# A long convolution and a gated feed-forward on one core: the second transform stage as sixteen array tiles, with a stored instruction order

## The chip, the cores and the metric

The kernel runs on one core of one Trainium2 chip. The time is the device time of one execution, in microseconds (us). Before the change it was 329.91 us, the median of three runs (324.05 to 332.69).

The core has five engines with a queue each, run in order: TensorE (PE in the profile; PEld are its weight loads), VectorE (DVE), ScalarE (ACT), GpSimd (POOL) and SyncE (SP). PE writes to PSUM, eight banks of 512 float32 per partition; the kernel uses them as four tiles of two banks. DMAs are issued from the queues of SP, ACT and POOL.

## What is computed

2048 positions, 640 channels, F = 1728. Inputs and output are bfloat16. `B_x` is not used.

```python
x = A_q
k_shift[s] = sum over t of k[s - t] * shift_k[:, t]        # 4 taps per channel
kv = k_shift * v
y  = irfft(rfft(pad(kv)) * rfft(pad(ssm_k)))[:2048]        # causal long convolution, per channel
y  = y + kv * ssm_D
h  = x + layernorm(x) * y
g, u = silu(layernorm(h) @ w_gate), layernorm(h) @ w_up
out = h + (g * u) @ w_down
```

## The kernel before

**Blocks.** The sequence is cut into four blocks of 512 positions (`j` = 0 to 3). Position 4p + b of a block lies in partition p, column group b, so a block is four row groups (`b`) of 128 partitions. The channels are cut into two halves (`c`) of 320 columns (`CW`). The convolution is done block against block by a transform of 1024 points, so that output block j is the sum over i of the spectrum of x-block i times the spectrum of filter block j - i. The feed-forward part of block j needs the whole convolution of block j.

**Block 0** (`dense_c`): both transforms are dense. `dense_h` multiplies by 128x128 matrices from a table of 2 MB (`den`), eight matmuls of 320 columns for each of four frequency groups `h`; `products` and `combine` make the complex product on DVE, and eight more matmuls per `h` transform back.

**Blocks 1 to 3** (`conv_c`): `kv_block` makes the taps and the product with v on DVE, eight instructions of 1280 columns per half. `fwd` is the first transform stage (two 128x128 matmuls per `b`), whose result goes through four SBUF-to-SBUF DMAs that regroup the partitions. `spec` (with `stage2`) is the second stage: per `h` and operand four matmuls of 128 rows by 64 columns. `shift_add` (two DVE instructions of 640) adds the spectrum of the filter block before. `products` multiplies the complex spectra, with pairs of 1280-column instructions for each term and adds between the terms; `combine` and, in block 3, two further adds finish real and imaginary parts. `inv2` is the inverse second stage (64 rows by 128 columns), followed by an evacuation, a regrouping DMA (`rs`) and the inverse first stage in `conv_bp`, which also multiplies with the normalised x, adds x and takes the statistics of the second layernorm. Each `evac` of 640 columns from PSUM may run on ACT or DVE.

**Feed-forward.** `ffn_pair` multiplies by `WG` and `WU` (540 matmuls of 512 columns over the four blocks), takes silu on ACT and the product on DVE straight from PSUM. `ffn_b` multiplies by `WD` (448 matmuls of 320 columns); for blocks 0 and 1 x is added on PE by 16 identity matmuls (`RESPE`) and the result evacuated, for blocks 2 and 3 DVE adds it.

**Order.** `P.op` only lists the operations with a priority and an estimated cost. `Prog.schedule` then walks a simulated clock and fixes the order on each engine, and for operations that ACT or DVE may do, the engine; `emit` writes the five queues with their semaphore waits. Loads of blocks 1 to 3 and of the weights are issued on POOL's queue (`load_kv`, `load_x`, `load_weights`); a weight piece waits until the piece two before it has landed, and the first ones until `kv_last[0, 0]`, the last tap instruction of block 0. `KIN` and `VIN` have one buffer each, so the load for a next half waits for the instructions that read the one before. The regrouping DMAs are on SP's queue. For blocks 1 to 3 the filter is turned by a DMA transpose through DRAM.

All PE operations but transposes are recorded by the helper in line 559, all DVE two-operand instructions by line 756, evacuations by 542 (with a scale: 545), DMA issues by line 550; silu is line 1103, normalisation 876 and 877, the layernorm sums on ACT 889 and 896, the power on POOL 867.

Of the kernel before, what the change touches and what calls it, by code (L numbers as in the profile page):

```python
# [40 lines left out]
class Prog:  # L41
    ENG = ("pe", "act", "dve", "pool", "sp")
    FRESH = {"pe": 0.22, "act": 0.145, "dve": 0.125, "pool": 0.15, "sp": 0.1}
    OVERLAP = {"pe": 0.0, "act": 0.105, "dve": 0.085, "pool": 0.0, "sp": 0.0}
    WIN = 3.41333

# [62 lines left out]
    def pe_end(self, t, c):  # L109

        w = self.clock
        while c > 1e-12:
            k = int((t + 1.7 + 1e-7) // self.WIN)
            while w["k"] < k:
                u = w["busy"].get(w["k"], 0.0) / self.WIN
                if w["s"] == 1.0:
                    if u < 0.55 and w["k"] > 8:
                        w["s"] = 0.5
                elif u >= 0.83:
                    w["s"] = 1.0  # L120
                w["k"] += 1
            e = (k + 1) * self.WIN - 1.7
            if e - t < 1e-9:
                e += self.WIN
            d = min(c / w["s"], e - t)
            w["busy"][k] = w["busy"].get(k, 0.0) + d
            t += d
            c -= d * w["s"]
        return t

    def schedule(self, dma_model, bias):
        self.clock = {"k": -1, "s": 1.0, "busy": {}}
        pemode = 0
        free = {e: 0.0 for e in self.ENG}
        order = {e: [] for e in self.ENG}
        ready = []
        for o in self.ops:
            o.ready = o.minready
            if o.npred == 0:
                ready.append(o)  # L140
        dmafree = [0.0]
        t = 0.0
        left = len(self.ops)
        while left:
            done_any = True
            while done_any:
                done_any = False
                for e in ("pe", "dve", "act", "sp", "pool"):
                    if free[e] > t + 1e-9:
                        continue  # L150
                    best, held = None, set()
                    for o in sorted((o for o in ready if e in o.engs and o.ready <= t + 1e-9), key=lambda o: (o.prio, o.idx)):
                        c = o.engs[e]
                        if e == "dve" and "act" in o.engs:
                            if max(t, free["act"]) + o.engs["act"] <= t + c + bias:
                                continue
                        if e == "act" and "dve" in o.engs:
                            if max(t, free["dve"]) + o.engs["dve"] + bias < t + c:
                                continue
                        ok = True  # L160
                        want = {}
                        for tl in o.tiles:
                            if tl.live:
                                continue
                            pl = self.pools[tl.pool]
                            n = want.get(tl.pool, 0)
                            if pl.inorder and (pl.at + n >= len(pl.seq) or pl.seq[pl.at + n] is not tl):
                                ok = False
                                break
                            if tl.pool in held:  # L170
                                ok = False
                                break
                            want[tl.pool] = n + 1
                        if not ok:
                            continue
                        for pn, n in want.items():
                            if sum(1 for f in self.pools[pn].free if f[0] <= t + 1e-9) < n:
                                ok = False
                                if n > 1:
                                    held.add(pn)  # L180
                        if ok:
                            best = o
                            break
                    if best is None:
                        continue
                    o = best
                    done_any = True
                    ready.remove(o)
                    left -= 1
                    for tl in o.tiles:  # L190
                        if not tl.live:
                            pl = self.pools[tl.pool]
                            pl.free.sort(key=lambda f: f[0])
                            _, tl.base, tl.prev = pl.free.pop(0)
                            tl.live = True
                            if pl.inorder:
                                pl.at += 1
                    o.eng, o.start = e, t
                    if o.dma is None:
                        c = o.engs[e] - self.OVERLAP[e]  # L200
                        if e == "pe":
                            c += 0.105 if o.mode != pemode else 0.0
                            pemode = o.mode
                        o.finish = self.pe_end(t, c) if e == "pe" else t + c
                        free[e] = o.finish
                    else:
                        free[e] = t + o.engs[e]
                        o.finish = dma_model(o, free[e], dmafree)
                    o.pos = len(order[e])
                    order[e].append(o)  # L210
                    for tl in o.tiles:
                        tl.touch.append(o)
                        tl.left -= 1
                        if tl.left == 0 and tl.pool is not None:
                            self.pools[tl.pool].free.append((max(p.finish for p in tl.touch) + 0.14, tl.base, tl.touch))
                    for s in o.succ:
                        s.npred -= 1
                        k = s.deps[o]
                        if k == 0 or (e == "pe" and "pe" in s.engs):
                            fin = o.finish  # L220
                        else:
                            fin = o.finish + max(self.FRESH[x] for x in s.engs)
                        s.ready = max(s.ready, fin)
                        if s.npred == 0:
                            ready.append(s)
            nxt = [f for f in free.values() if f > t + 1e-9] + [o.ready for o in ready if o.ready > t + 1e-9]
            for pl in self.pools.values():
                nxt += [f[0] for f in pl.free if f[0] > t + 1e-9]
            if not nxt:
                if left:  # L230
                    raise RuntimeError("stuck: " + "; ".join(
                        f"{o.name}[{','.join(x.name for x in o.tiles if not x.live)}]" for o in ready[:20]))
                break
            t = min(nxt)
        self.order = order
        self.span = max(o.finish for o in self.ops)

    def emit(self, nc, es, block, ndma_sems):
        sems = {e: es.enter_context(nc.semaphore("s_" + e)) for e in self.ENG}
        dsem = [[es.enter_context(nc.semaphore(f"s_d{i}")), 0, None, i < ndma_sems[0]] for i in range(sum(ndma_sems))]  # L240
        glob = sorted(self.ops, key=lambda o: (o.start, o.idx))
# [102 lines left out]
def _tables(R):  # L344
    N = 256 * R
    I1 = 64 // R
    q = np.arange(128)[:, None]
    s1f = np.zeros((128, 2, 128))
    for T in range(2):
        f1 = (64 * T + np.arange(64))[None, :] + 0.5  # L350
        s1f[:, T, 0:64] = np.cos(2 * np.pi * q * f1 / 256)
        s1f[:, T, 64:128] = -np.sin(2 * np.pi * q * f1 / 256)
    s1i = np.stack([s1f[:, T, :].T for T in range(2)], axis=1)
    w2 = np.zeros((2, R, 128, 2, 64))
    w2i = np.zeros((128, R, 2, 128))
    for T in range(2):
        for G in range(R):
            for i in range(I1):
                f1 = 64 * T + R * i + G + 0.5
                for m in range(R):  # L360
                    col = i * R + m
                    for b in range(R):
                        r0, r1 = i * R + b, 64 + i * R + b
                        th = 2 * np.pi * b * (f1 + 256 * m) / N
                        w2[T, G, r0, 0, col] = np.cos(th)
                        w2[T, G, r1, 0, col] = np.sin(th)
                        w2[T, G, r0, 1, col] = -np.sin(th)
                        w2[T, G, r1, 1, col] = np.cos(th)
            w2i[T * 64:(T + 1) * 64, G, 0, :] = w2[T, G, :, 0, :].T
            w2i[T * 64:(T + 1) * 64, G, 1, :] = w2[T, G, :, 1, :].T  # L370
# [33 lines left out]
def bass_sequential_preLN__ssm_conv_h3__swiglu_ffn__prompt_kernel(  # L404
# [27 lines left out]
    with ExitStack() as es:  # L432
# [98 lines left out]
        def dve4(n):  # L531
            return 0.274 + 0.00026 * n
# [706 lines left out]
```

## Time and profile before

One profiled execution had a span of 329.1 us; the median of the plain runs is 329.91 us.

| engine | busy us | share | instructions |
|---|---|---|---|
| PE | 284.9 | 87% | 1724 |
| DVE | 251.0 | 76% | 441 |
| ACT | 184.7 | 56% | 293 |
| POOL | 40.8 | 12% | 55 |

| instructions | count | mean ns |
|---|---|---|
| DVE 128x1280 bf16, SBUF operands | 176 | 824 |
| DVE 128x640 bf16, SBUF operands | 96 | 485 |
| DVE 128x320 bf16, SBUF operands | 16 | 318 |
| DVE 128x1024 from PSUM | 24 | 1221 |
| DVE 128x640 from PSUM | 20 | 818 |
| ACT evacuation 128x640 | 148 | 701 |
| ACT normalisation, 320 / 640 columns | 28 / 12 | 647 / 916 |
| DVE normalisation, 320 / 640 columns | 4 / 4 | 360 / 463 |

A busy time counts each instruction from its start to its modelled end. Matmuls overlap, so the mean of one (386 ns for 512 columns) is longer than the distance from one start to the next. In lists in order of time, a row is a run of instructions of one kind: start, time from the first start to the last end, engine, line, operation, and how many (x8). In a table by stretches each engine has its busy us and number of instructions, then come the granted PE clock (1.00 is full), the share of the DMA engines and GB/s.

### The profile page before, as it was taken

The numbers are of one execution on the slowest core, as the hardware profiler recorded it, in microseconds if no ns is written. First come the engines' busy times: TensorE is split into PE (matmuls) and PEld (weight loads), VectorE is DVE, ScalarE is ACT, GpSimd is POOL, SyncE is SP. The second block draws the span as 40 slices with busy tenths as digits, with TensorE's granted clock in tenths as the row PEclk, the third lists the DMA queues.
The fourth block names the chain that finished last, engine by engine and source line by source line (L and its number), as shares of the span: only waits on it lengthen the run. The fifth ranks groups of instructions, "written<-read, shape, count | busy, mean of one in ns | idle before, by whom it ended". The sixth has DMA issues, their size and how long they took to land.

```text
span 329.1 us, 4717 instructions
## 1 busy us (share of the span) xinstructions
PE 284.9 (87%) x1724; PEld 151.7 (46%) x1740; DVE 251.0 (76%) x441; ACT 184.7 (56%) x293; POOL 40.8 (12%) x55
## 2 busy tenths in 40 slices
PE   3999773787999999999989971648999999999996
PEld 1567441443444366644436640223444477444474
DVE  1969997579799999699999799998499955222322
ACT  4388986875658854875748462578755214112200
POOL 2513235321100202100010000021000001000000
PEclk9999795589899999999999995556999999999999
DMA  7998859989794533331111213321110111000011
GB/s 197 348 393 262 249 170 331 126 258 240 211 271 118 179 132 120 118 114 41 65 57 38 96 67 120 120 82 40 51 72 0 43 60 42 20 0 2 0 42 40
DMA packets 33099, 40.57 MB, mean 123 GB/s; under 512 B 10472, under 2 KB 28291, under 8 KB 33076
## 3 DMA queue, kind: packets, MB, share of 16 engines
q1 hardware_dynamic: 28932, 25.57, 25.4%
q0 software_dynamic: 3296, 14.01, 14.7%
q10 hardware_dynamic: 848, 0.69, 0.8%
q8 instruction: 14, 0.23, 0.3%
q14 instruction: 9, 0.07, 0.1%
HBM read 21.91 MB, written 4.59 MB: 81 GB/s over the span
## 4 chain that ended last, share of the span: by engine, by line
PE 40%; DVE 36%; DMA 15%; issue 4%; ACT 3%; POOL 2%; ACTq 0%; SPq 0%; POOLq 0%; DVEq 0%
PE ps L559 39%; DVE sb L756 33%; DMA sb<-sb 6%; DMA sb<-in_A_k_dram 6%; ACT sb L542 2%; DMA sb<-in_A_ssm_k_dram 2%; DMA sb<-in_B_w_gate_dram 2%; DVE stt L851 1%; POOL sb L550 1%; PE ps L656 1%; ACT sb L545 1%; DVE sb L1023 0%; POOL stt L867 0%; PE ps L1063 0%; POOL sb L666 0%
## 5 line engine op out<-in xcount | busy, mean ns | idle before, releaser
L559 PE MATMUL ps<-sb 128*128 128x320 bf16 (+2 forms) x1188 | 224.2, 343 | 9.4 <-DMA sb<-in_A_shift_k_dram 2.4
L756 DVE TENSOR_TENSOR sb<-sb 128x1280 bf16<-128x1280 bf16 (+1 forms) x288 | 181.2, 683 | 28.7 <-DMA sb<-in_A_k_dram 12.3
L559 PEld LDWEIGHTS ps<-sb 128*128 128x128 bf16 (+2 forms) x1204 | 116.6, 100 | 103.4 <-issue 10.9
L542 ACT ACTIVATE sb<-ps 128x640 bf16<-128x640 f32 (+1 forms) x131 | 90.4, 729 | 47.4 <-PE ps L559 41.6
L559 PE MATMUL ps<-sb,tab 128*64 128x320 bf16 (+2 forms) x432 | 62.0, 341 | 25.3 <-DMA sb<-sb 8.6
L756 DVE TENSOR_TENSOR sb<-ps,sb 128x1024 bf16<-128x1024 f32 (+3 forms) x52 | 50.2, 982 | 42.2 <-PE ps L559 40.0
L559 PEld LDWEIGHTS ps<-sb,tab 128*64 128x64 f16 (+2 forms) x432 | 26.7, 110 | 59.2 <-issue 22.1
L1103 ACT ACTIVATE sb<-ps 128x1024 bf16<-128x1024 f32 (+2 forms) x32 | 29.3, 916 | 43.6 <-PE ps L559 43.3
L877 ACT ACTIVATE sb<-sb,stt 128x320 bf16<-128x320 bf16 (+1 forms) x40 | 27.3, 728 | 14.4 <-DVE stt L869 11.9
L867 POOL TENSOR_TENSOR stt<-stt 128x2 f32<-128x2 f32 (+1 forms) x12 | 12.6, 1054 | 111.7 <-DVE stt L905 60.3
L545 ACT ACTIVATE sb<-ps 128x640 bf16<-128x640 f32 x24 | 15.6, 701 | 6.0 <-PE ps L559 6.0
L889 ACT ACTIVATE sb<-sb 128x640 bf16<-128x640 bf16 x16 | 11.9, 742 | 6.3 <-DMA sb<-in_A_q_dram 6.2
L896 ACT ACTIVATE sb<-sb,stt 128x640 bf16<-128x640 bf16 x16 | 13.2, 826 | 3.6 <-DVE stt L892 3.4
L851 DVE BATCH_NORM_STATS2 stt<-sb 128x6 f32<-128x320 bf16 x32 | 13.5, 477 | 0.0
L1063 PE MATMUL ps<-sb 128*128 128x128 bf16 x80 | 7.8, 265 | 3.7 <-DVE stt L869 3.1
L550 POOL DMA_DIRECT2D sb<-in_A_k_dram x6 | 5.9, 990 | 35.6 <-DVE sb L756 35.6
L550 POOL DMA_DIRECT2D sb<-in_A_v_dram x6 | 4.7, 775 | 45.5 <-PE ps L559 42.6
L1063 PEld LDWEIGHTS ps<-sb 128*128 128x128 bf16 x80 | 6.5, 120 | 6.0 <-ACT sb L877 3.6
L656 PE MATMUL ps<-sb 128*128 128x128 bf16 (+1 forms) x24 | 4.1, 282 | 2.6 <-DMA sb<-in_A_ssm_k_dram 2.6
L550 POOL DMA_DIRECT2D sb<-in_B_w_down_dram x6 | 4.3, 724 | 15.3 <-DMA sb<-in_B_w_down_dram 11.9
L656 PEld LDWEIGHTS ps<-sb 128*128 128x128 bf16 (+1 forms) x24 | 2.0, 118 | 5.2 <-DMA sb<-in_A_ssm_k_dram 3.2
L543 DVE COPY sb<-ps 128x1280 bf16<-128x1280 bf16 x3 | 2.5, 818 | 2.4 <-PE ps L1063 2.4
(24 smaller groups left out, 37.5 us busy)
## 6 DMA issues: line engine op xcount, KB each, us to landing
sb<-sb SPq DMA_DIRECT2D x72, 160.0 KB, 2.2
sb<-in_A_k_dram POOLq DMA_DIRECT2D x6, 560.0 KB, 6.3
out_dram<-sb SPq DMA_DIRECT2D x16, 160.0 KB, 1.8
sb<-in_B_w_gate_dram POOLq DMA_DIRECT2D x5, 416.0 KB, 5.5
sb<-in_B_w_up_dram POOLq DMA_DIRECT2D x5, 416.0 KB, 6.5
sb<-cst_den SPq DMA_DIRECT2D x8, 256.0 KB, 7.1
sb<-in_A_q_dram POOLq DMA_DIRECT2D x3, 640.0 KB, 5.6
sb<-in_A_v_dram POOLq DMA_DIRECT2D x6, 320.0 KB, 4.1
```

The lines of the kernel that those rows point to most:

```text
L542: fns = {"act": lambda a: a.activation(out=dst(), in_=src(), func=ACTF.Copy), "dve": lambda v: v.tensor_copy(out=dst(), in_=src())}
L545: fns = {"act": lambda a: a.activation(out=dst(), in_=src(), func=ACTF.Copy, scale=scale), "dve": lambda v: v.tensor_scalar(out=dst(), in0 ...
L550: fns = [(lambda g, d=d, s=s: g.dma_start(d(), s())) for d, s in subs]
L559: return lambda t: t.matmul(o(), l(), r(), start=st, stop=sp)
L756: return lambda v: v.tensor_tensor(out=o(), in0=a(), in1=b_(), op=op)
L851: vec(dve1(CW, False), lambda v: v.bn_stats(st6(l, j, b, c), V(xt, b * D + c * CW, CW)), [(xt, (b, c))], [(ST, ("s", l, j, b, c))], prio, ...
L867: P.op({"pool": 1.05}, lambda g: g.tensor_tensor(out=y, in0=va, in1=stt[:, 420:420 + hi - lo], op=ALU.pow), c1 + [(ST, "half")], c3, prio, ...
L877: "act": lambda a: a.activation(out=dst(), in_=src(), func=ACTF.Identity, scale=rs(l, j, b), bias=tmv(l, j, 3)[:, b:b + 1])},
L889: P.op({"act": act_c(D) + 0.22}, lambda a, b=b, jt=jt: a.activation(out=V(jt, 0, D), in_=V(xt, b * D, D), func=ACTF.Copy, accum_out=tmv(l, ...
L896: P.op({"act": act_c(D) + 0.3}, lambda a, b=b, jt=jt: a.activation(out=V(jt, 0, D), in_=V(xt, b * D, D), func=ACTF.Square, bias=tmv(l, j, ...
L1063: fns.append(lambda t, k=k, d=d: t.transpose(B16(pt, k, d * 128, 128), V(hn[k], d * 128, 128), V(IDN, 0, 128)))
L1103: P.op({"act": act_c(n)}, lambda a: a.activation(out=dst(), in_=src(), func=ACTF.Silu), rd, wr, -1000, name=f"si{j}{i}")
```

## The change

The computation is the same. What differs:

- **Second stage as 32x32 tiles.** `spec` now runs in rounds of sixteen matmuls, each of 32 rows by 32 columns of the array, 320 columns of data, four frequency groups in the four row strips, four results in the four column strips; each row strip writes a PSUM bank of its own. For the filter of blocks 1 to 3 a second round accumulates the filter block before with other weights (`oWP`) into the same PSUM, which takes the place of `shift_add`. The table is laid out so that real and imaginary parts lie in neighbouring partitions.
- **Sums of products in PSUM.** `swap` copies a spectrum with neighbouring partitions exchanged (two DMAs on SP). `product` is one 1280-column DVE instruction; each term needs two, one with the swapped operand. `inv2` runs one round per product and accumulates all terms in PSUM, which takes the place of the adds in `products` and of `combine`. In block 2 a second accumulation is made ahead for block 3 (`keep`), and in block 3 added at the evacuation (`added`, on DVE).
- **Block 0 like the others.** `dense_c`, `dense_h` and the 2 MB table are gone. For block 0 alone `kv_first` loads k whole, transposes it on PE, and does the taps as 24 matmuls per `b` with diagonal matrices (`diag`, 512-column DVE instructions) accumulated in PSUM; one DVE product with v per `b` follows.
- **Smaller moves.** `KACC`: in blocks 2 and 3 the three adds of `kv_block` are accumulating DMAs on POOL's queue. `UPACT`: in blocks 0 to 2 ACT copies u out of PSUM, and DVE multiplies from SBUF. `RESPE` is off: DVE adds x. `norm` is always on DVE. The first layernorm of block 0 is done with DVE statistics, not ACT. The first weight load waits for `kv_last[0, 0]`, now the second of the four products of `kv_first`.
- **Order from a table.** `schedule` is gone; `replay` reads `_PLAN`, a text with each operation's number, engine, start, duration and PSUM pool, and fixes the orders from it.

```diff
-        def shift_add(dst, do, cur_, co, prv, po, hs, prio, nm):
...
+        def tiles(outs, wt, src, st, sp):
+            return [mm(lambda r=r, q=q: outs(r, q), lambda r=r, q=q: wt(r, q), lambda r=r, q=q: src(r, q), st, sp) for r in range(4) for q in range(4)]
+
+        def spec(nm, us, prev, hp, dst, off, prio):
+            pa, pb_ = P.tile("p2", "pC"), P.tile("p2", "pC")
+
+            def o_(g, q):
+                return ps[32 * q:32 * q + 32, (pa, pb_)[g // 2].base + (g % 2) * 512:(pa, pb_)[g // 2].base + (g % 2) * 512 + CW]
...
+            fns = rnd(oWX, us, True, prev is None)
...
+            if prev is not None:
+                fns += rnd(oWP, prev, False, True)
...
+        def swap(src, off, prio, nm):
+            t = P.tile("sw" + nm, "E")
+            dma([(lambda r=r: sb[r:128:2, t.base:t.base + 1280],
+                  lambda r=r: sb[1 - r:128:2, src.base + off * 640:src.base + off * 640 + 1280]) for r in range(2)],
+                164, [(src, off), (src, off + 1)], [(t, 0), (t, 1)], prio, name=f"sw{nm}", kind="shuffle")
+            return t, 0
...
+        def product(a, b_, prio, nm):
+            (ta, oa), (tb_, ob) = a, b_
+            p = P.tile("P" + nm, "PP")
+            vec(dve2(1280), tt(lambda: V(p, 0, 1280), lambda: V(ta, oa * 640, 1280), lambda: V(tb_, ob * 640, 1280), ALU.mult),
...
+        def inv2(pts, ps_, hp, st, sp, prio, reserve, nm):
...
+            for i, (p, w) in enumerate(ps_):
+                fns += tiles(o_, lambda q, g, w=w: tb(w + (hp * 4 + g) * 32, 32, 32 * q, 32 * q + 32),
+                             lambda q, g, p=p: V(p, g * CW, CW, 32 * q, 32 * q + 32), st and i == 0, sp and i == len(ps_) - 1)
...
+            Ws = swap(*W, pr, f"W{nm}{hp}")
...
+            Xs = swap(*X, pr, f"X{nm}{hp}") if j else None
...
+            t0 = (old(SXt, 0), W, old(SXt, 0), Ws) if j else (X, W, X, Ws)
+            if j == 0:
+                Hs = run([[t0]], plain, "m")
             else:
...
+                t1 = (X, old(SKt, 0), Xs, old(SKt, 0))
+                if j == 2:
+                    X1s = swap(*old(SXt, 1), pr, f"Y{nm}{hp}")
+                    t2 = (old(SXt, 1), old(SKt, 1), X1s, old(SKt, 1))
+                    Hs = run([[t0, t1], [t2]], plain, "m")
+                    run([[(old(SXt, 1), W, X1s, W), (X, old(SKt, 1), Xs, old(SKt, 1))]], keep, "a")
+                else:
+                    Hs = run([[t0, t1]], added if j == 3 else plain, "m")
...
             def add():
+                if KACC[j]:
+                    dma([(lambda: V(t0, 0, W4), lambda: V(t1, 0, W4))], 328, [(t0, 0), (t1, 0)], [(t0, 0)], prio, eng="pool", name=f"kva{j}{c}",
+                        kind="acc")
+                    return
...
+                if UPACT[j]:
+                    ub = P.tile("ub", "UB")
+                    P.op({"act": act_c(1024)}, lambda a: a.activation(out=V(ub, 0, 1024), in_=B32x2(u, 512), func=ACTF.Copy),
...
-        P.schedule(dma_model, 0.8)
...
+        P.plan = _plan(_PLAN, P)
+        P.replay(P.plan)
```

## The prediction

> **What bounds the kernel now.** I read the busy times first, then the same by stretches between the starts of the feed-forward parts, then the shapes, the chain of waits, and rows in order of time for distances between matmuls.
>
> ```profile
> PE 284.9 (87%) x1724; PEld 151.7 (46%) x1740; DVE 251.0 (76%) x441; ACT 184.7 (56%) x293; POOL 40.8 (12%) x55
> ```
>
> No engine is full over the span, so the bound changes by stage. The stretches:
>
> ```profile
> 64.90:84.90 20.00, 16.78 (x81) 7.19 (x81) 16.18 (x25) 12.33 (x19) 3.54 (x5) 0.84 0.99 247
> 84.90:139.00 54.10, 52.52 (x355) 28.32 (x358) 49.00 (x84) 37.26 (x54) 5.78 (x6) 1.00 0.53 159
> 139.00:197.50 58.50, 54.94 (x335) 28.62 (x336) 56.34 (x86) 36.92 (x63) 3.58 (x4) 1.00 0.20 69
> 197.50:229.70 32.20, 17.31 (x93) 7.86 (x95) 29.40 (x60) 19.15 (x35) 4.08 (x5) 0.52 0.26 92
> 229.70:283.80 54.10, 53.53 (x341) 28.98 (x344) 37.32 (x71) 24.31 (x34) 1.41 (x2) 1.00 0.12 44
> ```
>
> From 139 to 230 us DVE is full (56.34 of 58.50, then 29.40 of 32.20). PE runs out of work at 196, falls to a clock of 0.52, and waits for block 2's convolution. In the last stretch PE is full. The last feed-forward, to 326 us, is PE alone.
>
> ```profile
> L756 DVE TENSOR_TENSOR sb<-sb 128x1280 bf16<-128x1280 bf16 x176 | 140.3, 824 | 20.1 <-DMA sb<-in_A_k_dram 12.3 <-PE ps L559 6.1 <-ACT sb L542 0.5
> ```
>
> These 176 are the taps, products and adds that fill DVE. The last view is PE in order of time:
>
> ```profile
> 133.26 0.72 PE L1063 MATMUL ps<-sb 128*128 128x128 bf16 x10
> 133.82 1.52 PE L559 MATMUL ps<-sb 128*128 128x320 bf16 x10
> 135.17 0.72 PE L1063 MATMUL ps<-sb 128*128 128x128 bf16 x10
> 135.73 1.25 PE L559 MATMUL ps<-sb 128*128 128x320 bf16 x8
> 136.91 0.83 PE L559 MATMUL ps<-sb,tab 64*128 64x320 bf16 x8
> ...
> 142.10 0.73 PE L559 MATMUL ps<-sb,tab 128*64 128x320 bf16 x8
> 142.77 1.25 PE L559 MATMUL ps<-sb 128*128 128x512 bf16 x5
> ...
> 144.62 1.25 PE L559 MATMUL ps<-sb 128*128 128x512 bf16 x5
> 145.71 0.57 PE L559 MATMUL ps<-sb,tab 128*128 128x320 bf16 x3
> ```
>
> Starts give prices at full clock: five of 512 columns take 145.71 - 144.62 = 1.09, so 0.218 each; ten of 320 take 135.17 - 133.82 = 1.35, so 0.136; ten of 128, 0.056. The eight on half the array's columns (128*64) take 0.67, four times 0.136 plus 0.13: two run side by side, and leaving the shape costs 0.13. Entering costs 136.91 - 135.73 - 8 x 0.136 = 0.09.
>
> **DVE, removed and added** (0.824 per 1280 columns, 0.485 per 640, from the rows). Block 2: before 2 halves x (8 taps + 32 products and adds) x 0.824 + 24 x 0.485 = 77.6; after 2 x (5 + 20) x 0.824 = 41.2, so -36.4. Block 1: 2 x 20 x 0.824 + 16 x 0.485 = 40.7 against 2 x 16 x 0.824 = 26.4, so -14.3. Block 3: 44.6 against 2 x 13 x 0.824 + 8 x 0.82 (adding at the evacuation) = 28.0, so -16.6. Block 0 loses 16 taps, 16 of 640 and 16 of 320 columns (26.1) and gains 8 products, 4 from PSUM, 8 statistics (0.477) and 5 diagonals (at 0.68, the 512-column row from PSUM): 17.1, so -9.0. Normalisation comes over from ACT: 28 x 0.36 + 12 x 0.463 = +15.6. The gate product from SBUF is 1024/1280 x 0.824 = 0.66 instead of 1.221, 18 times: -10.1. Adding x: 8 x 0.818 = +6.5. Sum -64: DVE from 251 to about 187, or some 10 more if a dozen evacuations go to it. ACT loses 27.3 of normalisation and about 7.9 of sums, and gains 18 copies at 1.02: about 168 plus a few evacuations. Neither is now the longest.
>
> **PE after block 0.** Feed-forward: 540 x 0.218 + 448 x 0.136 = 178.6. First stages both ways of blocks 1 to 3: 144 x 0.136 = 19.6. Transposes: 60 x 0.056 = 3.4. Tiles: per half 14 rounds of sixteen in blocks 1 and 3, 26 in block 2, so 108 rounds (124 with block 0). No row shows sixteen tiles at once. At the low end a round is one stream, 0.136; at the high end every load and matmul pair has a place of its own, as in the transposes, 16 x 0.056 = 0.90. I take 0.16, near the low end, because the row nearest to it, the half-array one, shows its two tiles side by side, and because these weight loads start close together:
>
> ```profile
> 80.81 0.14 PEld L559 LDWEIGHTS ps<-sb,tab 128*64 128x64 f16 x4 [2.69 <-DMA sb<-sb]
> ```
>
> Four loads that take 106 ns each lie within 0.14, so they start some 0.01 apart, and 16 x 0.01 = 0.16. That makes 108 x 0.16 = 17.3, plus 44 changes of shape in and out, 44 x 0.22 = 9.7. Total 228.6. Before, the same stretch held 178.6 + 19.6 + 3.4 + 2.2 for adding x, 144 half-array pairs at 0.136 = 19.6, and 72 groups at up to 0.22 = 15.8: 239. So PE itself gains only 10, most of it uncertain.
>
> The Trainium skill, "TensorE: Matmul & The Clock Gate", section "Back-to-back issue gap", speaks against the change: a matmul starts no sooner than about 25 ns after the one before, however small. Taken for tiles, a round is 0.40 and the result 297 + 108 x 0.24 = 323. The same page's section on row and column tiling gives about 4 ns between tiles, which is below my 0.01; no run here shows sixteen.
>
> **When PE can start on the feed-forward.** Before: 64.90, the first matmul of 512 columns. After, two paths. Data: k lands at about 8.5 (the first filter load, of half its size, lands at 7.4); 20 transposes and two evacuations of 1.24 to 12.3; the four groups of 24 diagonal matmuls at 2.6 with the clock still low, then 1.4, and the product to 21.5; first stage 1; regrouping DMA 4 to 5 (median 2.2, but beside the loads the chain shows 5.45 and 7.14); second stage with two evacuations 1.9; two products 1.65; inverse and two evacuations 2; DMA 3.5; inverse first stage to statistics 5; the other half 4 behind: about 46. Layernorm, transposes and evacuation 5 by the sum of the rows, 14 in the trace of before (51 to 64.9), because other work stands between: 51 to 60. Weights: the first goes after the second product, at about 18; the first pair took 8.5, the four later ones 5.3 each: 48, plus up to 5 while POOL's queue stands at the load of block 1's second half, which waits for the one KIN buffer. I take 54, with 48 and 65 as ends. The loads shrink by the 2 MB dense table, which helps here alone: in the first 16.5 us the DMA share is 0.94.
>
> **What is hidden, and by what.** The 16 swaps per half add 64 issues to SP's queue (160 with the regroupings, 72 before), up to 0.85 each: 54 us of a queue that has 300; behind them stand regroupings, filter transposes and stores. Each puts one DMA (2.2 to 7.1) into the chain of a half block. The cover is the feed-forward of the block before (44.7) on PE; without it three blocks pay 2 to 7 each. The 12 accumulating DMAs wait on POOL's queue for DVE's tap product, ahead of weight pieces, next loads and the power of the layernorm. No row shows one; between the 4.3 of the store of 320 KB and the 12.05 of the slowest load of k, three in a row are 13 to 36 per half, and the halves share one pair of TMP buffers: 34 to 80 per block. Block 2 has from about 55 to 135 for it. Hidden, unless near the upper end; then 10 to 20.
>
> The skill's "TensorEngine Tiling (Array Packing)", "PSUM Bottleneck", warns that tiling speeds up PE and not the evacuation; here evacuations go from 148 to 172, at 701 ns in ACT's row. That would be 17 us of ACT time, which has room.
>
> **Sum.** By PE: 54 + 228.6, less 5 of block 1's first stages done before 54, over 0.96 (array time found in the stretches after 229.70: 51.4 + 40.9 of 96) = 287, + 3.2 from the last matmul to the end (326 to 329.1) = 290. By difference: 329.1 - 10.9 (earlier start) - 10 (PE) - 23.5 (the stretch from 197.50: 17.31 busy at half clock is 8.7 of work in 32.2) = 285. Neither holds a loss like that of the first feed-forward, whose 20.0 us before hold 12.6 of array time. I add those 7 to the first sum: 297. The plain runs stand at 329.91 beside the span of 329.1, so nothing is added for that.
>
> **Rivals.**
> - *A round is bound by issue* (slower). Sixteen loads and sixteen matmuls at the transposes' pace: 108 x (0.90 - 0.16) = 80, so 377. For it: no row shows more than two tiles. Against: the row of four loads. Slower by 2% from a round of 0.52 (297 + 108 x 0.36 = 336). Chance 0.10.
> - *The feed-forward starts no earlier.* POOL's queue and the layernorm's waits stay: 297 + 11 = 308; if the loss there doubles too, 315. For it: 14 us for 5 us of work before. Chance 0.20.
> - *The convolution still ends last.* Three DMAs in a row, accumulating loads at their upper end, or queues fixed by wrong durations leave PE the hole of block 2: 297 + 23.5 = 320; with 10 to 17 more at block 3, up to 337. Against: DVE falls by 36 in just that block. Chance 0.13, about half of it over 323, and 0.01 over 336.
> - *All hidden*: the start at 48 and 0.98: 48 + 223.6 / 0.98 + 3.2 = 279. Chance 0.07.
>
> The forecast's own case, 285 to 306, has the other 0.50. 282 to 322 holds all but the first rival, half the third and most of the fourth: about 0.8. A measurement of this kernel tells about 2% from no change (323.3 to 336.5; the runs before spread by 2.6%). Faster is the own case, the late start, half the third rival and the last: 0.83. Within 2% is the rest of the third, 0.06. Slower 0.11.
>
> **What would show it.** Sixteen-tile rounds about 0.16 apart; DVE near 190 to 200 busy; the first 512-column matmul near 54; no stretch at half clock after it; PE over 0.93 busy from there. Wrong if rounds stand 0.4 or more apart, if PE waits for DMAs or DVE before a feed-forward, or if POOL's queue holds weights back past 60.

## The result, and the profile after

The changed kernel takes 348.79 us (median of 4 runs, 345.9 to 353.53) against 329.75 us for the kernel before beside it: a ratio of 1.0692, with a 95% interval of 1.0567 to 1.0816. The prediction was 297 us, range 282 to 322. The profiled execution took 347.39 us, its span is 345.5 us. Times are medians of all executions of a kernel, which differ among themselves by 1 to 4%; ratios and their intervals use its faster executions alone, and the profiled executions of `e6`, `e7`, `e8` and `e10` are of the slower kind.

The page of the kernel after: busy times, the granted clock by slices of 8.6 us, the DMA engines' share by slices, the chain that ended last by engine, the row of the small tiles, and the two kinds of SBUF-to-SBUF transfer (median us from issue to landing last).

```profile
PE 276.2 (80%) x3366; PEld 144.6 (42%) x3392; DVE 204.2 (59%) x356; ACT 174.2 (50%) x260; POOL 47.7 (14%) x64
...
PEclk9995555655899999999999999856799999999999
DMA  7869999999889749448464324662351200100001
...
PE 48%; DMA 26%; ACT 9%; DVE 9%; issue 4%; SPq 3%; ACTq 0%; DVEq 0%; POOLq 0%
...
L434 PE MATMUL ps<-sb,tab 32*32 32x320 bf16 (+1 forms) x2176 | 81.8, 348 | 51.4 <-DMA sb<-sb 25.4
...
sb<-sb SPq DMA_DIRECT2D x160, 160.0 KB, 3.9
sb<-sb POOLq DMA_DIRECT2D x12, 320.0 KB, 4.5
```

DVE is relieved (251.0 to 204.2) and PE has a little less to do, as intended. But PE stood still for 51.4 us ahead of the small tiles, and half of that was ended by SBUF-to-SBUF transfers; they are 21% of the chain that ended last, 6% before. There are 160 of them on SP's queue instead of 72, and the middle one takes 3.9 us instead of 2.2. The clock is at half for most of the time from 27 to 88 us, and the DMA engines are nearly full until some 90 us.

The same kernel by stretches (us, length, then busy time of PE, PEld, DVE, ACT, POOL, granted clock, DMA share, GB/s). The cuts are the first 512-column matmul of each feed-forward, and the last store of block 1 at 217.7:

```profile
0.00:92.40 92.40, 49.86 (x736) 23.52 (x738) 57.47 (x111) 53.61 (x87) 22.55 (x37) 0.69 0.96 277
92.40:152.60 60.20, 55.14 (x648) 29.75 (x655) 41.28 (x70) 32.33 (x42) 11.41 (x12) 0.97 0.72 192
152.60:217.70 65.10, 59.75 (x875) 31.55 (x881) 40.89 (x64) 41.27 (x65) 8.21 (x9) 1.00 0.48 149
217.70:243.30 25.60, 14.50 (x301) 7.15 (x303) 16.16 (x33) 17.02 (x31) 2.59 (x3) 0.64 0.52 166
```

Two things are to be seen. The first feed-forward starts at 92.4 us (before: 64.9), with the DMA engines 0.96 busy up to there. And between block 1's last store and the third feed-forward there is still a hole of 25.6 us, against 30.7 us before. The forecast had put it down to DVE; now DVE is busy in only 16.16 us of it.

The distances between the starts of the feed-forwards, in us, are the measure for all that follows (a kernel's row adds up to its span; the hole is counted from the issue of block 1's last store):

| kernel | to 1st | 1st to 2nd | 2nd to 3rd | 3rd to 4th | 4th to end | hole before 3rd |
|---|---|---|---|---|---|---|
| before | 64.9 | 73.0 | 87.3 | 55.8 | 48.1 | 30.7 |
| after | 92.4 | 60.2 | 90.7 | 52.2 | 50.0 | 25.6 |
| before, block 0 by stages (`e5_old_tiled_start`) | 91.6 | 67.2 | 82.2 | 55.0 | 48.1 | 25.2 |
| after, other order (`e8_new_order`) | 76.0 | 80.1 | 74.4 | 53.6 | 47.7 | 3.6 |
| after, other order, weights earlier (`e9_weights_earlier`) | 79.8 | 70.7 | 75.2 | 56.4 | 47.5 | 4.7 |
| after, longer transfer times (`e10_order_b`) | 95.0 | 65.9 | 77.4 | 56.4 | 47.5 | 13.1 |
| after, longer transfer times (`e11_order_c`) | 87.8 | 65.2 | 87.5 | 57.4 | 47.6 | 23.1 |
| after, dense block 0, other order (`e12_dense_start`) | 56.7 | 100.3 | 72.1 | 54.7 | 47.7 | 4.0 |

After against before: +27.5 to the first, -12.8, +3.4, -3.6 and +1.9, together +16.4. All of the loss arises before the first feed-forward, and the gain hoped for between the second and the third did not come. In the chain of waits through the hole two SBUF-to-SBUF transfers take 3.88 and 5.79 us; the rest are products on DVE, evacuations on ACT and matmuls that wait for one another.

The last view is the chain of waits before the first feed-forward (start, duration, what; pieces left out):

```profile
26.78 5.19 DMA sb<-sb
...
37.85 8.06 DMA sb<-sb
...
53.80 5.64 DMA sb<-sb
...
61.12 7.59 DMA sb<-sb
...
70.54 10.35 DMA sb<-sb
...
81.35 0.84 PE ps L434 x31
...
82.86 4.62 DMA sb<-sb
...
90.77 1.38 PE ps L434 x96
...
92.43 2.75 PE ps L434 x12
```

Six transfers, one behind another, make 41.5 of the 66 us from 26.78 to 92.43. By their places in SP's order the first three belong to block 0 (two regroupings of its values, one swap), the last three to block 1, whose work stands in front of block 0's layernorm in PE's fixed order: block 0's last statistics are done at about 79 us, its feed-forward starts 13 us later.

### The profile page after: what moved, and what is told of

Same layout as the page of the kernel before. It is cut to its first block, busy times and chain, and to the rows that moved or that the text cites. A ratio compares the mean times of both kernels' runs of the same rounds, so it can differ in the third digit from the quotient of the medians.

```text
span 345.5 us, 8043 instructions
## 1 busy us (share of the span) xinstructions
PE 276.2 (80%) x3366; PEld 144.6 (42%) x3392; DVE 204.2 (59%) x356; ACT 174.2 (50%) x260; POOL 47.7 (14%) x64
## 3 DMA queue, kind: packets, MB, share of 16 engines
q0 software_dynamic: 5024, 17.94, 20.4%
## 4 chain that ended last, share of the span: by engine, by line
PE 48%; DMA 26%; ACT 9%; DVE 9%; issue 4%; SPq 3%; ACTq 0%; DVEq 0%; POOLq 0%
PE ps L434 46%; DMA sb<-sb 21%; ACT sb L416 7%; DVE sb L637 7%; SPq L425 3%; DMA sb<-in_A_ssm_k_dram 2%; DMA out_dram<-sb 1%; ACT sb L419 1%; DMA sb<-in_A_q_dram 1%; ACT sb L721 1%; DVE stt L683 1%; DVE sb L417 1%; PE ps L887 1%; PE ps L535 1%; ACT sb L928 0%
## 5 line engine op out<-in xcount | busy, mean ns | idle before, releaser
L434 PE MATMUL ps<-sb 128*128 128x512 bf16 (+4 forms) x1066 | 192.4, 334 | 5.8 <-ACT sb L928 2.6
L637 DVE TENSOR_TENSOR sb<-sb 128x1280 bf16<-128x1280 bf16 (+3 forms) x152 | 110.1, 762 | 50.8 <-DMA sb<-sb 21.8
L434 PEld LDWEIGHTS ps<-sb 128*128 128x128 bf16 x1092 | 98.9, 98 | 85.7 <-issue 6.3
L434 PE MATMUL ps<-sb,tab 32*32 32x320 bf16 (+1 forms) x2176 | 81.8, 348 | 51.4 <-DMA sb<-sb 25.4
L434 PEld LDWEIGHTS ps<-sb,tab 32*32 32x32 f16 (+1 forms) x2176 | 35.6, 92 | 99.8 <-issue 39.9
L637 DVE TENSOR_TENSOR sb<-ps,sb 128x640 bf16<-128x640 f32 (+3 forms) x50 | 42.1, 846 | 58.7 <-PE ps L434 57.2
L942 ACT ACTIVATE sb<-ps 128x1024 bf16<-128x1024 f32 x18 | 18.5, 1025 | 21.8 <-PE ps L434 15.5
L695 DVE TENSOR_SCALAR sb<-sb,stt 128x320 bf16<-128x320 bf16 (+1 forms) x48 | 16.8, 391 | 5.3 <-PE ps L887 3.1
L425 POOL DMA_DIRECT2D sb<-sb x12 | 10.9, 909 | 51.6 <-DVE sb L637 45.9
L417 DVE CAST sb<-ps 128x640 bf16<-128x640 f32 x12 | 9.8, 822 | 10.3 <-PE ps L434 10.3
```

Of the source, the lines that this page charges most:

```text
L417: "dve": lambda v: v.tensor_copy(out=dst(), in_=src())}
L425: fns = [(lambda g, d=d, s=s: g.dma_start(d(), s(), **kw)) for d, s in subs]
L434: return lambda t: t.matmul(o(), l(), r(), start=st, stop=sp)
L637: return lambda v: v.tensor_tensor(out=o(), in0=a(), in1=b_(), op=op)
L695: vec(dve4(n), lambda v: v.tensor_scalar(out=dst(), in0=src(), scalar1=m, scalar2=rs(l, j, b), op0=op, op1=ALU.mult), reads + [(ST, cell), ...
L942: P.op({"act": act_c(1024)}, lambda a: a.activation(out=V(ub, 0, 1024), in_=B32x2(u, 512), func=ACTF.Copy), [(u, 0), (u, 1)], [(ub, 0)], - ...
```

## The experiments

Theory A at the outset: the transfers that the change adds to the start, each slow beside the loads, set the start. Rival B: the stored order is at fault, which was laid out for shorter transfers (`_PLAN` gives a regrouping or swap before 90 us 2.1 to 4.3 us).

**Fewer bytes beside the start.** Weight loads cut to about a quarter, in the new kernel and in the old. The feed-forwards use the loaded part again.

```diff
-  V(t, i * FM, FM),  dram(wd, i * 128 * F, [[F, 128], [1, FM]])
+  V(t, i * FM, 256), dram(wd, i * 128 * F, [[F, 128], [1, 256]])
-  V(w, d * st + col, 128)
+  V(w, d * st + col % 256, 128)
```

> The changed kernel with about three quarters of the weight bytes left out (the gate and up loads fetch 256 of 1664 columns, the down loads one of two or three row groups; the matmuls read what was fetched, so the output is not the reference's; the instructions, their order and their waits stay). Theory A (the start is bound by DMA hops that share the DMA engines with the loads): the first 512-column matmul comes at 70 to 80 us instead of 92.4, total 325 to 338. Theory B (the stored order on PE, with block 1's work ahead of block 0's end, sets it; DMA sharing is not the matter): 90 to 92 and 344 to 349.

> The same weight bytes left out of the kernel before (output not the reference's). Control: if A is right and the old block 0 goes without hops, it gains less than the changed kernel does, 4 to 10 us of 329.8 (first 512-column matmul 56 to 62 instead of 64.9). If both gain the same, the shared DMA engines are a cost of either kernel and do not explain the difference.

New: 334.8 us (ratio to the kernel before 1.0206, 1.0079 to 1.0333), first 512-column matmul 79.5 us. Old: 323.58 us (0.9955, 0.9907 to 1.0004), at 61.5. The same bytes cost the new kernel 14 us and the old one at most 4 (by the ratio 1.5, and its interval includes none): the new start moves by 12.9 us with them, the old one by 3.4. Theory A holds for the start of both; the old kernel's gain in time lies below the 4 to 10 us that it named.

**Swaps left out.** The products that should read swapped rows read unswapped ones.

```diff
-            t = P.tile("sw" + nm, "E")
-            dma([(lambda r=r: sb[r:128:2, ...], lambda r=r: sb[1 - r:128:2, ...]) for r in range(2)], ...)
-            return t, 0
+            return src, off
```

> The changed kernel without its 64 swap DMAs: the product with exchanged partitions reads the unexchanged operand, so that part of the complex product is left out. Theory A (hops on SP's queue): 318 to 332, and the regrouping DMAs in the start land 1 to 3 us sooner. Theory B or swaps hidden by the feed-forward: 343 to 349.

338.53 us (1.0427, 1.0343 to 1.0512), first 512-column matmul 86.1 us. Ten us less, between the two theories; the hole before the third feed-forward is 22.6 us, so the swaps are not what makes most of it.

**Transposing transfers made plain.** The filter of blocks 1 to 3 arrives unturned.

```diff
-  g.dma_start_transpose(out=V2(t, 0, CW, 4, CW), in_=dram(A_ssm_k, c * CW * S + B * j, [[S, CW], [1, B]]))
+  g.dma_start(V2(t, 0, CW, 4, CW), dram(A_ssm_k, c * CW * S, [[S, 128], [CW, 4], [1, CW]]))
```

> The changed kernel with the six transposing DMAs of the filter replaced by plain DMAs of the same bytes (so the filter of blocks 1 to 3 is not turned and the output is not the reference's). Theory A, in the form that regroupings stand in SP's ring behind the transposes (one regrouping behind the fourth took 10.35 us): 335 to 342. If the transposes only cost their bytes: 345 to 349.

339.41 us (1.0443, 1.036 to 1.0525), first 512-column matmul 86.2 us: as theory A had it.

**All three at once.**

> The new kernel with three edits at once that were made singly before: weight loads cut to about a quarter, the 64 swaps left out (products take the unswapped spectrum), and the six transposing transfers made plain ones of the same bytes. The result is not the reference's. Theory A (slow hops on SP's queue are the loss; each edit takes away other hops' delays): the three gains nearly add, 14 + 10 + 9, first 512-column matmul 62 to 72 us, time 308 to 320 us. Rival B (they free the same wait, and the rest is the fixed order or the longer chain of block 0 itself): first 512-column matmul 75 to 82 us, time 324 to 334 us.

326.07 us (0.9989, 0.9926 to 1.0053), first 512-column matmul 80.3 us, second to third feed-forward 89.7 us. Theory A falls here: singly the three gave 14, 10 and 9 us, together 23, and a start that is no earlier than with light weights alone (79.5). They free in part the same wait, as rival B of this run had it. Even without these transfers the start is 15 us behind the kernel before, and block 2's hole stays (23 us).

**Block 0 by stages in the kernel before.** One part of the change alone.

```diff
-                conv_c(j, c) if j else dense_c(c)
+                conv_c(j, c)
-            shift_add(kt, ko, st, so, pv, po, hs, pr, f"{nm}{h0}")
+            if j:
+                shift_add(kt, ko, st, so, pv, po, hs, pr, f"{nm}{h0}")
-                    den_piece(("f", h), ...); den_piece(("i", h), ...)
```

> The kernel before, with block 0 alone put through its own two-stage transform (second stages on half the array's columns, no swaps, no accumulating transfers), and the dense table and its 2 MB left out; its planner orders the work anew. Theory A (what costs the new kernel its start is that block 0's chain now goes through regrouping transfers beside the loads, whatever the second stage's shape): the first 512-column matmul moves from about 62-65 to 75-92 us and the whole by +8 to +25 us (335 to 352), since nothing after the start is changed. Rival B (block 0's transform is not the cost; the new kernel's order, fixed beforehand with too short durations, and the swaps are): the first 512-column matmul stays within 60 to 70 us, the whole within 322 to 333 us, as 2 MB of loads fall away.

348.14 us (1.0748, 1.0672 to 1.0825): the whole loss of the change, without a single tile, swap or accumulating transfer. Its start, by stretches and in its chain of waits:

```profile
0.00:91.60 91.60, 54.75 (x260) 17.57 (x262) 59.08 (x106) 66.94 (x114) 25.20 (x38) 0.78 0.88 263
```

```profile
18.78 9.15 DMA sb<-sb
...
27.98 0.76 PE ps L557 x4
28.76 0.70 ACT sb L540
...
45.31 5.95 DMA sb<-sb
...
68.46 0.76 PE ps L557 x4
...
69.74 4.71 DMA sb<-sb
...
75.13 2.14 DMA sb<-sb
```

Four transfers make 22 us of this chain, and between them PE and ACT take turns (0.76 us for a stage, 0.70 for its evacuation) where the dense way had no transfer at all. So block 0's way through the stages is enough for a loss of this size, in the order that the old scheduler makes of it. The rest of the change, with the stored order, adds nothing to that and takes nothing off: 348.8 against 348.1.

**Accumulating transfers back on DVE** (`KACC` false for all blocks, the 12 additions at the same places of the order).

> The new kernel with the 12 accumulating transfers of blocks 2 and 3 as additions on VectorE (12 x 0.82 = 9.9 us more on it), at their places in the same order. If those transfers are hidden, as the prediction took them: 345 to 352 us, no change or up to +4. If three in a row of 4.5 us hold block 2's convolution: 336 to 343 us, and the stretch between the third and fourth feed-forward (197.5 to 248 us in the new kernel) is shorter by 5 us or more.

The four times lie from 336.1 to 348.96 us and give no interval; in the profile the first feed-forward starts at 97.5 us, the second to the third takes 88.3 us against 90.7, and the hole before the third is 23.2 us against 25.6. They are not what makes most of the hole; whether they cost a few us is open.

**The same operations in another order.** Only the stored table differs: loads that block 0 does not need are held back, and block 2's convolution comes earlier.

```diff
-_PLAN = """ 225,2,0,32 0,1,0,370 15,4,0,408 ...
+_PLAN = """ (the same operations, other places)
```

> The new kernel with every operation as it is and another order of them on the engines and queues: up-weights held back to about 47 us, block 1's filter and value loads to about 34 and 54 us, block 0's work first, block 2's convolution work earlier. Theory A (the number of hops, each 4 to 10 us beside the loads, sets the start whatever the order): first 512-column matmul 85 to 95 us, wait before the third feed-forward 20 us or more as now (217.7 to 243.3), time 340 to 355 us. Rival B (the order is what fails: it puts loads and block 1's work in front of block 0's hops, and block 2's convolution too late): first 512-column matmul 70 to 80 us, wait before the third feed-forward under 15 us, time 312 to 330 us.

329.13 us (1.0098, 1.0054 to 1.0142): of a loss of 6.9% some 1% is left, with every operation kept. The profiled execution, of 333.64 us, has these stretches from the first feed-forward on:

```profile
76.00:156.10 80.10, 70.81 (x888) 35.19 (x889) 53.66 (x90) 38.84 (x54) 17.38 (x19) 0.90 0.87 228
156.10:226.90 70.80, 66.18 (x1086) 33.32 (x1084) 59.03 (x101) 46.80 (x74) 11.21 (x12) 0.98 0.66 196
226.90:230.50 3.60, 2.89 (x82) 1.70 (x82) 3.27 (x6) 2.78 (x6) 0.00 (x0) 1.00 0.48 178
```

Rival B holds for both places, but most of the gain is at the second: the hole before the third feed-forward is 3.6 us instead of 25.6. The second feed-forward starts no earlier than in the changed kernel (156.1 against 152.6): up-weights held too long stop the 512-column matmuls of the first one from about 85 to 92.4 us.

**Three more orders.** Up-weights earlier; then two orders laid out with longer transfer times.

> The re-ordered kernel, laid out again with one edit: the up-weights are held to 28 us instead of 47. In the re-ordered kernel block 0's layernorm was ready at about 76 us and the last up-weight landed at 92.3. If that weight is what ends last there, and loads that start earlier do not slow block 0's transfers by as much: the feed-forward of block 0 runs without its pause (84.5 to 92.4 us), time 316 to 325 us. If the loads and block 0's transfers share one limit, what one gains the other loses: first 512-column matmul 80 to 92 us, time 326 to 336 us.

> The same operations in a further order, chosen with longer times for transfers: block 1's load of x held to 51 us, block 2's first load to 71 us, up-weights to 49. If the order in the start is what is left: first 512-column matmul 74 to 90 us, with no pause after it for weights, third feed-forward by 222 us, time 314 to 324 us. If the start is bound by the bytes of weights and block 1's loads, whatever the order: 326 to 336 us.

> The same operations in a third order: gate-weights held to 23 us and up-weights to 28, block 2's filter loads to 114 us. Same two readings as for the order before: 314 to 325 us if order is what is left, 326 to 336 us if the start is bound by bytes.

331.32 us (1.0129, 1.0007 to 1.0251), 341.16 us (1.0352, 1.0144 to 1.056) and 347.22 us (1.0625, 1.0504 to 1.0746), first 512-column matmul at 79.8, 95.0 and 87.8 us. None is below the kernel before. The first has the time of the reading "share one limit"; the other two lie above both of their ranges, and the hole before the third feed-forward is 13.1 and 23.1 us in them. In the first of the three, the chain before the first feed-forward is

```profile
57.14 3.81 DMA sb<-in_B_w_up_dram
60.95 0.29 issue
61.24 5.36 DMA sb<-in_B_w_up_dram
66.59 0.29 issue
66.89 5.31 DMA sb<-in_B_w_gate_dram
72.19 0.29 issue
...
72.55 0.72 issue
73.27 1.60 POOL stt L708 x2
```

POOL's queue waits for weight after weight, and block 0's layernorm needs that queue for its power (line 708). The statistics that the power reads are ready at 70.5 and 71.4 us, so its wait there is 2 to 3 us. That such an order gives to block 0's transfers what it takes from the weights is a reading of this chain; no run tests it.

**Block 0 dense again, in the new kernel.** Block 0's output as before the change; its spectra, which later blocks need, by tiles behind that.

```diff
-            for c in range(2):
-                conv_c(j, c)
+            if j == 0:
+                for c in range(2):
+                    dense_c(c)
+                for c in range(2):
+                    spectra0(c)
+            else:
+                ...
```

> The new kernel with block 0's output made as in the kernel before (the dense tables, 2 MB, no transfers between its steps) and block 0's spectra, which later blocks need, made by tiles behind that; blocks 1 to 3 as in the new kernel; all of it in an order laid out anew with transfer times near the measured ones. Theory A (what cost the new kernel its gain is block 0's chain of transfers, then the order; tiles in blocks 1 to 3 are a gain): first 512-column matmul 54 to 66 us, third feed-forward by 218 to 226 us (re-ordered kernel: 225.7 and 230.5), time 314 to 324 us. Rival B (block 1's convolution and the loads are the bound of the start, whatever block 0's way): the first feed-forward starts as early, but the second no earlier than about 150 us, and the time is 326 to 334 us, as with order alone.

333.56 us (1.0246, 1.0183 to 1.0309). The first two stretches:

```profile
0.00:56.70 56.70, 46.09 (x393) 32.04 (x394) 40.76 (x102) 21.17 (x30) 12.20 (x24) 0.97 0.82 241
56.70:157.00 100.30, 77.76 (x1091) 38.06 (x1091) 75.53 (x121) 62.31 (x99) 19.91 (x24) 0.91 0.72 218
```

The first feed-forward starts 36 us earlier than in the changed kernel, and the second at 157.0 us, later than its 152.6. Rival B of this run holds: an early start is worth nothing when block 1's convolution is not ready. What in block 1 holds it was not tried. The trace shows one place, of some 3 us: on DVE a product of block 2, which waits for a transfer that lands at 149.31 us, stands in front of block 1's layernorm, whose statistics are done at 147.4.

**What is left in the better order.** The same three edits as above, on the order with the earlier up-weights.

> The kernel of the run with earlier up-weights, weight loads cut to about a quarter (the feed-forwards use the loaded part again). Its chain of waits before the first 512-column matmul (79.8 us) is weight loads from 57 to 72 us. If the weights' bytes and their place on POOL's queue set its start: first 512-column matmul 62 to 72 us, second feed-forward by 141 us, time 314 to 323 us. If block 0's transfers set it by themselves: 75 to 80 us, time 326 to 332 us.

> The kernel of the run with earlier up-weights, the 64 swaps left out (products take the unswapped spectrum). In the stored order the same edit moved the first 512-column matmul by 6 us and the whole by 10. If the better order already hides the swaps: first 512-column matmul 77 to 80 us, time 327 to 332 us. If the swaps cost the start whatever the order: 70 to 76 us, time 318 to 326 us.

> The kernel of the run with earlier up-weights, the six transposing transfers made plain ones of the same bytes. In the stored order the same edit moved the first 512-column matmul by 6 us and the whole by 9. If the better order already hides them: first 512-column matmul 77 to 80 us, time 327 to 332 us. If they hold SP's queue whatever the order: 70 to 76 us, time 319 to 326 us.

| edit | stored order: from 348.79 us | better order: from 331.32 us |
|---|---|---|
| light weights | 334.8 (-14) | 321.85 (-9.5), ratio 0.9884 (0.9813 to 0.9955) |
| no swaps | 338.53 (-10) | 326.61 (-4.7), ratio 0.9955 (0.9895 to 1.0015) |
| plain for transposing | 339.41 (-9) | 329.45 (-1.9), ratio 1.0105 (1.0058 to 1.0151) |

First 512-column matmuls at 73.9, 77.3 and 76.0 us. Light weights land in the first range in time, but neither in the start (62 to 72) nor in the second feed-forward (143.0, not by 141). Without swaps the start is in the "hidden" range and the time between the two; with plain transfers the time is in the "hidden" range and the start at the end of the other. The kernel before took 329.41 us beside the better order and 326.22 beside these three, so the ratios are the safer measure: from 1.0129, with its interval of 1.2% either way, they fall by 2.5%, 1.7% and 0.2%, some 8, 6 and 1 us. Weight bytes still cost in the better order, swaps perhaps half of what they did, and for the transposing transfers no cost is left that these runs can tell from none.

## Why the prediction was wrong

**The step that failed most: "When PE can start on the feed-forward", 54 us.** It was 92.4, outside the ends of 48 and 65. The weights' path was about right (48 plus up to 5; the last of the five large up-weight pieces landed at 56.1, the small last pieces at 59.8 and 60.8). The data path was not. It counted two transfers for a half block ("regrouping DMA 4 to 5", "DMA 3.5") and "the other half 4 behind". The chain has six, of 4.6 to 10.4 us. Three mistakes are in this: the price, which was that of transfers without much beside them; the second half, whose regroupings of the values land at 42.4 to 52.4 us, the first half's at 30.7 to 32.0, so 12 to 20 us behind and not 4; and the order, in which half of the six belong to block 1. 41.5 us less the 7.5 to 8.5 counted is 33 to 34 us, beside the 38 missed; as the two chains do not hold the same steps, this is a comparison and not a share. The Trainium skill, "DMA: Bandwidth & Descriptors", section "Anatomy of one DMA", gives a transfer issued by GpSimd about 2.0 us plus its bytes over 436 GB/s. Taken for those on SP's queue, that is an estimate of 2.4 for 160 KB; it fits the median of 2.2 us of the kernel before and not the 4.6 to 10.4 in this start. Its section "Issuing engines are not separate DMA queues" says that transfers issued from different engines share the same DMA engines, and the light weights, on another queue, agree: 14 us.

**"What is hidden, and by what".** The swaps were put behind the feed-forward of the block before. In the stored order they cost 10 us, 6 of them before the first feed-forward, where there is no feed-forward to hide them. In the better order they cost 4.7. By the ratios that is some 6, with an interval of about 4 either way. The accumulating transfers have the predicted price (4.5 us, forecast 4.3 to 12.05) and do not make most of block 2's hole.

**"By difference ... 23.5".** The forecast took block 2's hole for DVE's and dropped it with DVE's work. DVE's work fell, but the hole stayed at 25.6 us. It is laid out in the order itself. `_PLAN` holds a start and a duration for each operation, so the times that the order was made for can be read from it, before any run:

| kernel | a regrouping or swap, 24 to 90 us, median in the table | 1st feed-forward, table / measured | hole before 3rd, table / measured |
|---|---|---|---|
| after | 3.75 | 65.9 / 92.4 | 19.6 / 25.6 |
| `e8_new_order` | 4.87 | 69.3 / 76.0 | 3.5 / 3.6 |
| `e9_weights_earlier` | 4.56 | 70.7 / 79.8 | 4.4 / 4.7 |
| `e10_order_b` | 10.86 | 90.8 / 95.0 | 11.6 / 13.1 |
| `e11_order_c` | 8.44 | 84.9 / 87.8 | 20.4 / 23.1 |
| `e12_dense_start` | 5.29 | 52.6 / 56.7 | 3.7 / 4.0 |

Where the table has a large hole the trace has a large one, with the same operations on DVE in the first five rows. And the changed kernel's table itself starts the first feed-forward at 65.9 us, past the forecast's upper end of 65. Its 3.75 us for a transfer stands against a measured median of 6.0; tables with more than that (10.86, 8.44) were met more nearly in the start, but gave slow orders. The orders differ in more than these durations, so that longer or shorter ones make an order slow or fast is not shown. In the three orders with a small hole the second to the third feed-forward takes 72.1 to 75.2 us against 87.3 before; that the work taken from DVE is needed for this is likely, but no run has the old work in a new order. That the order comes from a stored table was known; it was only named ("queues fixed by wrong durations") inside a rival with a chance of 0.13.

**The form of the sum.** Start plus PE's work over 0.96 assumes that every later block is ready when PE is. `e12_dense_start` has the forecast's start (56.7 us) and takes 333.56.

**What was right.** The tiles. PE in order of time in the kernel after:

```profile
208.47 0.49 PE L434 MATMUL ps<-sb,tab 32*32 32x320 bf16 x32
208.89 1.26 PE L434 MATMUL ps<-sb 128*128 128x320 bf16 x8
...
212.57 0.90 PE L434 MATMUL ps<-sb,tab 32*32 32x320 bf16 x64
213.40 1.80 PE L434 MATMUL ps<-sb 128*128 128x320 bf16 x12
```

Two rounds with the change of shape take 0.42 us and four take 0.83; the forecast's 0.16 a round and 0.22 for the shape give 0.54 and 0.86. The first rival (a round bound by issue) falls with that, and so does a round of 0.40. The forecast's working (sixteen starts 0.01 apart) was not right: within a round the starts lie 3 to 4 ns apart (208.466 to 208.516 us for the sixteen), and a round lasts about one stream (the next starts at 208.612, 0.146 behind); that the two come out alike is luck. DVE ended at 204.2, 7 us over the upper of the two figures, which decides nothing.

**The rivals.** "The feed-forward starts no earlier" and "the convolution still ends last" came true together, the first far beyond its price (38.4 us against 11 to 18), the second within it: by the forecast's own reckoning the hole of 25.6 us, with 14.50 busy at a clock of 0.64, loses 16.3, against 23.5. The chances treated them as two cases of which one could happen. The forecast's own 297, plus 38.4 and 16.3, is 351.7, against the 347.39 us of the profiled execution.

**What stays open.** Whether an order exists that puts these operations below the kernel before: four orders gave 329 to 347 us. And what holds block 1's convolution when block 0 is early, but for the 3 us named above.

## What to carry to other kernels

Removing work from a busy engine pays only where the steps it waited for are also early: find who is late next, in the order that is really issued, and if that order is a stored table, read its own times for the holes that it already has, and lay it out again with transfer times near the measured ones before judging the change (two orders laid out with longer ones came out at 341 and 347 us here). Price an SBUF-to-SBUF transfer by the transfers that run beside it, and count how many stand in a row, those of other blocks on the same queue too. A chain of transfers at the very start of this kernel had no cover; the dense form without transfers, with 2 MB more to load, gave the earlier start there (56.7 us), though not the shorter time.

## What the hardware showed that was not expected

A 160 KB transfer from SBUF to SBUF took 2.5 us in the median before 24 us, 5.9 (up to 10.4) from there to 92.4 us, where the DMA engines are about full, and 2.2 in the kernel before over its whole span. Around one transposing transfer SP's queue itself stopped:

```profile
59.40 4.70 SPq L425 DMA_DIRECT2D sb<-sb  x6
64.15 6.28 SPq L504 DMA_TRANSPOSE sb<-in_A_ssm_k_dram  x1
70.54 1.21 SPq L425 DMA_DIRECT2D sb<-sb  x2
```

Its issue took 6.28 us, where six plain ones took 4.70 together, and the regroupings issued right behind it are the 10.35 us of the chain above. The other five transposing issues took 1.4 to 2.5 us. SP's queue was not alone: two weight pieces issued on POOL's queue at 67.18 and 68.79 us landed only at 79.5 and 80.7. Sixteen tiles of 32x32 stream side by side at about the price of one stream: two rounds, 32 matmuls of 320 columns, took 0.42 us with the change of shape.
